# Attention and gated MLP on one core: the order of the first loads and of the second head group, and four holds on GpSimd

## The chip, the core and the metric

The kernel runs on one core of a Trainium2 chip. The core has five engines with an instruction stream each: TensorE (PE) multiplies matrices, VectorE (DVE) and ScalarE (ACT) work elementwise, GpSimd (POOL) works elementwise and issues DMAs, and SyncE (SP) issues DMAs. Every engine executes its own stream in order and waits on semaphores for the others, so an instruction that waits holds back everything behind it on its engine. The metric is the time on the device in microseconds (us), as the median of several runs. Before the change it is 300.85 us, from six runs between 299.44 and 302.98.

## What is computed

Attention with normalised queries and keys is followed by a gated MLP. Shapes: batch 8, 12 heads, sequence 448, head dimension 64; model width 768, two halves of 512 in the MLP.

```python
q_n, k_n = rmsnorm(q, g_q), rmsnorm(k, g_k)         # x / sqrt(mean(x*x) + 1e-6) * g, over the head dimension
scores = (1 / sqrt(64)) * (q_n @ k_n.T)
attn = exp(scores - max) ; attn = attn / (sum(attn) + 1e-9)
x = concat_heads(attn @ v)                          # (8, 448, 768)
h = relu(x @ w_in) ; u, v = h[..., :512], h[..., 512:]
v_n = (v - mean(v)) / sqrt(var(v) + 1e-6)
v_s = einsum('ts,bsd->btd', w_spatial, v_n) + b_spatial
out = (u * v_s) @ w_out
```

## The kernel before, in words

**Groups.** The heads of a batch are split into three groups of four heads: group g of a batch takes heads g and g+3 of the first six and the same of the last six, so that all 128 partitions are used. There are 24 groups G in all: 0, 1, 2 are batch 0, and 3, 4, 5 batch 1. A group is 7 chunks of 128 columns per q and k, and its scores are 7 *passes*: pass p belongs to group p // 7.

**Loading.** `load_part(b, i, part, g)` (L101) issues one DMA for q (i = 0) or k (i = 1) of batch b. The data of one tensor and batch comes in five parts: part 0 the main rows of the first six heads, part 1 their tail, parts 2 and 3 the main rows of the last six in two partition halves, part 4 their tail. With `g` given, parts 0, 2 and 3 bring the two heads of one group only; without, six heads. Parts 1 and 4 always bring six heads. Batch 0 is loaded by groups, every later batch by five whole parts per tensor (`divmod(n, 5)` in L134 and L710). `load_v(b, parts)` (L111) issues the same five parts for v on GpSimd's queue, and `load_w_in(h)` (L186) four DMAs for one half of `w_in`, also on GpSimd. The buffers of two batches alternate: batch 1 has one of its own, batch 2 takes the place of batch 0 and of the early working tiles, once these are read for the last time.

**Preparing a group.** `squares(G, i)` (L223) squares q or k on GpSimd (or ScalarE), `reduce(G, i)` (L236) sums the squares on VectorE, `rstd(G)` (L244) takes the inverse root on ScalarE with two small instructions, `scaled(G, i)` (L252) multiplies q or k by it into bf16 on GpSimd or VectorE. Then the result is turned: by TensorE into PSUM with a copy out of it (`transpose_first` for group 0 in two halves, L283; `transpose_pe` for groups 1 to 5, L302), or by a DMA for later groups (L317), where k is then scaled by `k_scale` (L327). Group 0 is handled in two halves of 4 and 3 chunks (a third entry 0 or 1 in its key); the working tiles of halves come from the pool `first`.

**Scores and attention.** `scores` (L337) multiplies for one pass into PSUM; `expo` (L353) takes exponentials on ScalarE. `weigh(G, part)` (L367) multiplies the exponentials by ones (part -1) or by v (parts 0 and 1); `recip` (L383) and `xt_store` (L389) divide by the sum.

**Order.** The order on every engine is written out by hand. For passes 0 to 19 the loop at L680 issues `expo(p)`, transposes named in `TURN`, the scores of pass p + 1, and then what `early(p)` (L635) lists for that pass; `attend_late` (L404) spreads the attention of groups 0 and 1 over passes 10 to 13 and 15 to 18. From pass 20 on the loop at L750 works in steps of two passes with one exponential of double width; the first is step 10. What a step prepares stands in the table `todo`: it is filled from `EVEN`, `ODD` and `FIRST` (for groups 4 to 8) and with the loads of batches 2 and later. MLP work is filled in between the attention of later groups by a list of small units (`gated`, `fill`).

**The hold.** `after(key)` (L594) copies one element of a scaled tile on GpSimd. GpSimd thus waits there until the scaling has written it:

```python
def after(key):
    t = st_pool.tile([1, 1], BF, name="one")
    pool.tensor_copy(out=t, in_=nrm[key][0:1, 0, 0, 0:1])
```

Before the change it is called for both halves of group 0 and for group 1.

Of the kernel before, what the change touches and what calls it, by code (L numbers as in the profile page):

```python
# [11 lines left out]
BF = mybir.dt.bfloat16  # L12
# [7 lines left out]
def kernel(  # L20
# [24 lines left out]
    P = 128  # L45
    NG = 3
    NCH = 7
# [34 lines left out]
    raw, qbs = {}, {}  # L82

    def load_tile(b, i):
        pl = qb_pools[(b + 1) % 2] if b else first
        t = pl.tile([P, 2 * NG, NCH, D], FP, name="kb" if i else "qb")
        qbs[b, i] = t.rearrange("p h c d -> p h (c d)")
        for g in range(NG):
            x = t.rearrange("p (h g) c d -> p h g c d", g=NG)[:, :, g]
            raw[NG * b + g, i] = x  # L90
            if b == 0 and g == 0:
                raw[0, i, 0], raw[0, i, 1] = x[:, :, 0:4], x[:, :, 4:NCH]

    def pieces(x):

# [3 lines left out]


    def load_part(b, i, part, g=None, eng=sync):  # L101
        if part == 0 and (b, i) not in qbs:
# [8 lines left out]
    def load_v(b, parts):  # L111
        t = vts[b % 2].rearrange("p h c d -> p h (c d)")
        for i in parts:
            hs = slice(6, 12) if i > 1 else slice(0, 6)
            r, c, n, x = pieces(v[b][hs])[i]
            pool.dma_start(out=t[r, hs, D * c:D * (c + n)], in_=x)  # L116
# [9 lines left out]
    load_part(0, 1, 3, 0, act)  # L126
    load_part(0, 0, 4)
    load_part(0, 1, 4, None, act)
    for g in (1, 2):
        for i in (1, 0):  # L130
            for part in (0, 2):
                load_part(0, i, part, g)
    for n in range(10):
        load_part(1, *divmod(n, 5))  # L134


    ident = const.tile([P, P], BF)
# [48 lines left out]
    def load_w_in(h):  # L186
        w = w_in_v if h else w_in_u
        for l in range(4):
            pool.dma_start(
                out=w[32 * l:32 * l + 32, :, :],  # L190
                in_=moe_w_in[192 * l:192 * l + 192, DH * h:DH * h + DH].rearrange("(j p) f -> p j f", p=32))
# [31 lines left out]
    def squares(*key, eng=None):  # L223
        n = nch(key)
        if n == NCH:
            t = sq_pool.tile([P, 2, n, D], FP, name="sqt")
        else:
            t = first.tile([P, 2, n, D], FP, name=f"s{key[1]}{key[2]}")
        x = raw[key]
        if eng is act:  # L230
            act.activation(out=t, in_=x, func=AF.Square, bias=0.0, scale=1.0)
        else:
            pool.tensor_tensor(out=t, in0=x, in1=x, op=ALU.mult)  # L233
        sqt[key] = t

    def reduce(*key):  # L236
        n = nch(key)
        gk = (key[0],) + key[2:]
        if gk not in sqs:
            sqs[gk] = st_pool.tile([P, 2, 2 * n], FP, name=f"ms{n}")  # L240
        dve.tensor_reduce(out=sqs[gk][:, key[1], :], in_=sqt.pop(key).rearrange("p h c d -> p (h c) d"),  # L241
                          axis=AX.X, op=ALU.add)

    def rstd(*gk):  # L244
        t = sqs[gk]
        n = t.shape[-1]
        ln = st_pool.tile([P, 2, n], FP, name=f"ln{n}")
        rst[gk] = st_pool.tile([P, 2, n], FP, name=f"rs{n}")
        act.activation(out=ln, in_=t, func=AF.Ln, bias=eps, scale=1.0 / D)
        act.activation(out=rst[gk], in_=ln, func=AF.Exp, bias=0.0, scale=-0.5)  # L250

    def scaled(*key, eng=None):  # L252
        n = nch(key)
        if n == NCH:
            t = qn_pool.tile([P, n, 2, D], BF, name=f"n{key[1]}")
        else:
            t = first.tile([P, n, 2, D], BF, name=f"n{key[1]}{key[2]}")
        nrm[key] = t
        gk = (key[0],) + key[2:]
        (eng or pool).tensor_tensor(  # L260
            out=t.rearrange("p c h d -> p h c d"), in0=raw[key],
            in1=rst[gk][:, key[1], :].rearrange("p (h c) -> p h c", h=2).to_broadcast([P, 2, n, D]),
            op=ALU.mult)
# [19 lines left out]
    def transpose_first(i, y, eng):  # L283
        ps = ps_w.tile([P, 8, 128], BF, name="ps")
        if y == 0:
            t = first.tile([P, 512], BF, name=f"x{i}")
            turn(ps, 0, nrm[0, i, 0])
            (to_k if i else to_q)(t, ps, 4, eng)
        else:

            n = 3 if i else 4
            t = first.tile([P, 128 * n], BF, name=f"y{i}")
            if i == 0:
                turn(ps, 0, nrm[0, 0, 0][:, 3:4])
            turn(ps, n - 3, nrm[0, i, 1])
            (to_k if i else to_q)(t, ps, n, eng)
        if i == 0:
            qkt[0, 0, y] = t[:, 64 * y:64 * y + S]
        else:
            qkt[0, 1, y] = t  # L300

    def transpose_pe(G, i, eng):  # L302
# [309 lines left out]
    scaled(0, 1, 0, eng=dve)  # L612
    dve.tensor_copy(out=g2_col, in_=ps_g[:, 0:1])
    transpose_first(0, 0, act)
    squares(1, 0, eng=act)
    after((0, 1, 0))
    squares(1, 1)
    transpose_first(1, 0, dve)
    dummies(10)
    reduce(0, 1, 1)  # L620
    rstd(0, 1)
    reduce(1, 1)
    scaled(0, 0, 1, eng=dve)
    scaled(0, 1, 1, eng=dve)
    after((0, 1, 1))
    load_v(0, range(5))

    psp = {}

# [5 lines left out]
    def early(p):  # L635
        if p == 0:
            transpose_first(0, 1, dve)
            transpose_first(1, 1, dve)
            reduce(1, 0)
        elif p == 3:  # L640
            rstd(1)
            scaled(1, 0, eng=dve)
            scaled(1, 1, eng=dve)
            after((1, 1))
            squares(2, 1)
            load_w_in(1)
        elif p == 4:
            squares(2, 0, eng=act)
        elif p == 6:
            reduce(2, 1)  # L650
            reduce(2, 0)
        elif p == 8:
            rstd(2)
            scaled(2, 0, eng=dve)
            scaled(2, 1)
            squares(3, 0)
            squares(3, 1)
            load_v(1, range(5))
# [12 lines left out]
        if 10 <= p <= 13:  # L671
            attend_late(0, p - 10)
        if 15 <= p <= 18:
            attend_late(1, p - 15)
        if p in (0, 1, 2, 3, 4, 7, 8, 9, 14):
            dummies(6)

    TURN = {5: (1, 0), 6: (1, 1), 11: (2, 0), 12: (2, 1), 18: (3, 0), 19: (3, 1)}
    pass_scores(0)
    for p in range(2 * S0):  # L680
        expo(psp[p], p, 1)
        if p in TURN:
            transpose_pe(*TURN[p], dve)
        if p + 1 < 2 * S0:
            pass_scores(p + 1)
        early(p)
# [10 lines left out]
    todo = {}  # L697
# [8 lines left out]
                        todo.setdefault(s, []).append((what, G, i))  # L706
    for b in range(2, B):
        first_q = {2: S0, 3: 16}.get(b, (21 * b - 36) // 2)
        for n in range(10):
            todo.setdefault(first_q + n // (3 if b > 2 else 4), []).append(("ld", NG * b, n))  # L710

    ORDER = ("ks", "red", "rstd", "sc", "sq", "turn", "tr", "ld")

    def prep(s, early_act):
        for what, G, i in sorted(todo.get(s, ()), key=lambda x: (ORDER.index(x[0]), x[1:])):
            if (what == "rstd" and G < 5) != early_act:
                continue
            if what == "ld":
                load_part(G // NG, *divmod(i, 5))
            elif what == "turn":  # L720
                transpose_pe(G, i, dve)
            elif what == "sq":
                squares(G, i, eng=act if (G, i) in ((6, 1), (7, 1), (8, 1)) else None)
            elif what == "red":
                reduce(G, i)
            elif what == "rstd":
                rstd(G)
            elif what == "sc":
                scaled(G, i, eng=dve if (G, i) in ((4, 0), (5, 0)) else None)
            elif what == "tr":  # L730
                transpose_dma(G, i)
            elif what == "ks":
                k_scale(G)
# [86 lines left out]
```

## Time and profile before

| | |
|---|---|
| median of six runs | 300.85 us |
| the profiled execution: time / span of its trace | 301.68 / 299.8 us |
| busy: TensorE, VectorE, ScalarE, GpSimd | 92%, 70%, 68%, 67% of the span |
| data moved by DMA | 49.98 MB, 167 GB/s over the span |
| mean granted TensorE clock | 0.966 |

The profile page divides the span into 40 slices of 7.5 us; a digit is the busy share in tenths, 9 being 90% or more. "PEclk" is the TensorE clock that was granted, DMA the mean busy share of the core's 16 DMA engines:

```profile
PE   8675797979896999999999999999999999999994
DVE  3874355868746976996899686877897949644652
ACT  2687376597874787688677768867877876774421
POOL 3677299278994989958989989589989860400400
PEclk9799577999799999999999999999999999999999
```

Row by row: TensorE is almost full from the fourteenth slice (97.5 us) on, and has gaps before. In the fifth slice (30 to 37.5 us) ScalarE and GpSimd are at a few tenths, and TensorE's clock is granted at half. Bracketed remarks in later excerpts name the idle time of the engine just before an instruction and what ended it.

### The profile page before, as it was taken

To read this page: it belongs to the slowest core of one execution; us is meant where nothing else is said; L and a number is where in the kernel's file an instruction comes from. 1 tells how busy PE (TensorE), PEld (TensorE's weight loads), DVE (VectorE), ACT (ScalarE), POOL (GpSimd) and SP (SyncE) were. 2 spreads that over 40 slices of the span, in tenths; PEclk is the share of its full clock that TensorE was granted. 3 is DMA by queue.
4 is the path that set the end of the run, shared out by engine and by line. 5 is a ranking of instruction groups with operands and counts; after the bars stand their busy time and mean duration, and the time that the engine had idled before them with its cause. 6 is when DMAs were issued, how large, how long until landed. Compare 5 with 4: busy or idle time off the path is not lost.

```text
span 299.8 us, 6418 instructions
## 1 busy us (share of the span) xinstructions
PE 274.4 (92%) x2541; PEld 128.9 (43%) x2541; DVE 210.6 (70%) x363; ACT 204.7 (68%) x258; POOL 202.3 (67%) x188
## 2 busy tenths in 40 slices
PE   8675797979896999999999999999999999999994
PEld 8342233434342444444444444444344444444552
DVE  3874355868746976996899686877897949644652
ACT  2687376597874787688677768867877876774421
POOL 3677299278994989958989989589989860400400
PEclk9799577999799999999999999999999999999999
DMA  7999999447999999999979999999891794040145
GB/s 166 242 217 227 227 208 203 68 105 163 155 202 195 200 196 188 217 248 162 255 103 181 242 209 239 247 177 166 167 121 39 113 197 92 2 157 2 26 161 184
DMA packets 97120, 49.98 MB, mean 167 GB/s; under 512 B 67009, under 2 KB 93378, under 8 KB 97090
## 3 DMA queue, kind: packets, MB, share of 16 engines
q1 hardware_dynamic: 73986, 40.32, 64.2%
q0 software_dynamic: 21744, 8.66, 25.0%
q10 hardware_dynamic: 1360, 0.59, 0.8%
q8 instruction: 20, 0.33, 0.5%
q14 instruction: 10, 0.08, 0.1%
HBM read 38.55 MB, written 11.01 MB: 165 GB/s over the span
## 4 chain that ended last, share of the span: by engine, by line
PE 61%; DMA 13%; DVE 9%; ACT 8%; POOL 5%; issue 3%; SPq 0%; ACTq 0%; POOLq 0%; DVEq 0%
PE ps L379 13%; PE ps L458 11%; PE ps L530 10%; PE ps L488 9%; PE pss L350 8%; PE ps L498 7%; ACT et L357 5%; DMA kr<-n 5%; DMA vt<-in_v_dram 5%; DMA kb<-in_k_dram 3%; DVE ms L241 2%; DVE xt L393 2%; DVE kT L330 2%; PE pss L346 1%; POOL n L260 1%
## 5 line engine op out<-in xcount | busy, mean ns | idle before, releaser
L357 ACT ACTIVATE et<-pss 128x1792 bf16<-128x1792 f32 x74 | 123.0, 1663 | 51.2 <-PE pss L350 48.4
L393 DVE TENSOR_TENSOR xt<-ps,rc 128x448 bf16<-128x448 f32 x48 | 28.0, 619 | 35.7 <-ACT rc L386 31.3
L241 DVE TENSOR_REDUCE ms<-sqt 128x14 f32<-128x896 f32 x46 | 49.2, 1076 | 2.9 <-POOL sqt L233 2.5
L530 PE MATMUL ps<-w_out,gt 128*128 128x384 bf16 (+1 forms) x256 | 46.9, 327 | 0.9 <-DVE osb L435 0.4
L379 PE MATMUL ps<-et,vt 128*32 128x448 bf16 x768 | 44.0, 368 | 3.4 <-DMA vt<-in_v_dram 2.9
L458 PE MATMUL ps<-w_in_v,xt 128*128 128x512 bf16 (+1 forms) x192 | 45.6, 380 | 0.0
L260 POOL TENSOR_TENSOR n<-qb,rs 128x896 bf16<-128x896 f32 x18 | 30.4, 1687 | 21.0 <-ACT rs L250 17.2
L260 POOL TENSOR_TENSOR n<-kb,rs 128x896 bf16<-128x896 f32 x22 | 39.0, 1773 | 7.4 <-ACT rs L250 7.3
L350 PE MATMUL pss<-qT,kT 64*128 64x448 bf16 x254 | 37.5, 356 | 7.1 <-ACT et L357 4.4
L488 PE MATMUL ps<-xt,w_in_u 128*128 128x448 bf16 x192 | 40.1, 353 | 1.3 <-DVE vs L429 0.8
L233 POOL TENSOR_TENSOR sqt<-kb 128x896 f32<-128x896 f32 x20 | 33.6, 1682 | 6.7 <-DMA kb<-in_k_dram 6.5
L233 POOL TENSOR_TENSOR sqt<-qb 128x896 f32<-128x896 f32 x21 | 35.3, 1683 | 0.1
L530 PEld LDWEIGHTS <-gt 128*128 128x128 bf16 (+1 forms) x256 | 24.1, 101 | 21.1 <-issue 8.3
L435 DVE COPY osb<-ps 128x384 f32<-128x384 f32 (+1 forms) x46 | 25.1, 555 | 10.2 <-PE ps L530 9.2
L379 PEld LDWEIGHTS <-vt 128*32 128x32 bf16 x768 | 21.4, 100 | 21.4 <-issue 6.5
L116 POOL DMA_DIRECT2D vt<-in_v_dram x40 | 29.3, 738 | 0.0
L480 POOL TENSOR_SCALAR vn<-vs,nm,rv 128x512 bf16<-128x512 bf16 (+1 forms) x32 | 24.1, 769 | 7.2 <-issue 4.3
L498 PE MATMUL ps<-w_spT,vn 128*128 128x448 bf16 (+1 forms) x128 | 28.3, 365 | 0.2 <-DVE w_spT L209 0.2
L488 PEld LDWEIGHTS <-w_in_u 128*128 128x128 bf16 x192 | 17.3, 98 | 21.5 <-issue 7.6
L350 PEld LDWEIGHTS <-kT 64*128 64x128 bf16 x276 | 10.1, 94 | 37.3 <-issue 28.8
L458 PEld LDWEIGHTS <-xt 128*128 128x128 bf16 (+1 forms) x192 | 17.8, 100 | 18.3 <-issue 3.6
L330 DVE TENSOR_SCALAR_CACHE_REDUCE kT<-kr,g_col 128x896 bf16<-128x896 bf16 x18 | 20.5, 1136 | 4.1 <-DMA kr<-n 4.1
(86 smaller groups left out, 314.8 us busy)
## 6 DMA issues: line engine op xcount, KB each, us to landing
out_dram<-osb SPq DMA_DIRECT2D x24, 384.0 KB, 4.5
qb<-in_q_dram SPq DMA_DIRECT2D x7, 576.0 KB, 6.1
qb<-in_q_dram SPq DMA_DIRECT2D x14, 288.0 KB, 6.5
kb<-in_k_dram SPq DMA_DIRECT2D x7, 576.0 KB, 8.7
kb<-in_k_dram SPq DMA_DIRECT2D x14, 288.0 KB, 8.6
vt<-in_v_dram POOLq DMA_DIRECT2D x8, 288.0 KB, 6.0
vt<-in_v_dram POOLq DMA_DIRECT2D x16, 144.0 KB, 5.3
qb<-in_q_dram SPq DMA_DIRECT2D x20, 96.0 KB, 6.0
```

The lines of the kernel that those rows point to most:

```text
L116: pool.dma_start(out=t[r, hs, D * c:D * (c + n)], in_=x)
L233: pool.tensor_tensor(out=t, in0=x, in1=x, op=ALU.mult)
L241: dve.tensor_reduce(out=sqs[gk][:, key[1], :], in_=sqt.pop(key).rearrange("p h c d -> p (h c) d"), axis=AX.X, op=ALU.add)
L260: (eng or pool).tensor_tensor(out=t.rearrange("p c h d -> p h c d"), in0=raw[key], in1=rst[gk][:, key[1], :].rearrange("p (h c) -> p h c", ...
L350: pe.matmul(out=ps[:, h, 0:S], lhsT=kT[r, c0:c0 + 128], rhs=qT[r, :], start=True, stop=True, tile_position=(64 * h, 0))
L357: act.activation(out=ets[s][:, 2 * a:2 * a + 2 * m, :], in_=ps[:, 0:2 * m, 0:S], func=AF.Exp, bias=0.0, scale=1.0)
L379: pe.matmul(out=ps[32 * l:32 * l + 32, 0:S], lhsT=w, rhs=et_of(G, 3 if r == 3 else r + 4 * y, h), start=(r == 0), stop=(r == 3), tile_posi ...
L393: dve.tensor_tensor(out=xts[b][:, 2 * g + half, :], in0=pst.pop((G, half))[:, 0:S], in1=rec[G], op=ALU.mult)
L458: pe.matmul(out=ps[0:m, :], lhsT=xts[b][:, j, t0:t0 + m], rhs=w_in_v[:, j, :], start=(j == 0), stop=(j == 5), tile_position=(0, 0))
L488: pe.matmul(out=ps[:, 0:S], lhsT=w_in_u[:, j, 128 * f:128 * f + 128], rhs=xts[b][:, j, :], start=(j == 0), stop=(j == 5))
L498: pe.matmul(out=ps[:, 0:S], lhsT=vn_t[b % 2][0:kp, c, 128 * f:128 * f + 128], rhs=w_spT[0:kp, c, :], start=(c == 0), stop=(c == NT - 1))
L530: pe.matmul(out=ps[o:o + m, 0:384], lhsT=gts[b][f][:, t0:t0 + m], rhs=w_out[:, f, r], start=(f == 0), stop=(f == 3), tile_position=(0, o))
```

## The change

It has six parts, in the order of the program:

1. *Group 1 in halves.* Group 1 of batch 0 is now squared, summed, scaled and turned in two halves of 4 and 3 chunks, as group 0 was. Its first half is squared on ScalarE, q as well as k. A new helper, `transpose_half`, turns one half.
2. *Order of batch 0's loads.* Within group 1, k and q alternate by part; group 2 keeps tensor by tensor.
3. *v of batch 0 ahead of batch 1.* Two of the five v loads are issued before the second hold, the other three right behind it. Batch 1's q and k loads come later in the program, and the first of them has to wait for a one-element memset that GpSimd executes behind the second hold, ahead of the three v loads. SyncE's queue is in order, so all of batch 1 waits with it.
4. *Batches 1 and 2 by groups.* 22 loads per batch in place of 10: k and q of the batch's first group with the tails, then its second and third group.
5. *Passes 1 to 19 in a new order.* Scaling of group 2's and group 3's k goes from GpSimd to VectorE; `squares(2, 0)` goes from ScalarE to GpSimd; copies of the turned q of groups 2 and 3 go from VectorE to ScalarE, and both tensors of a group are turned in the same pass (13 and 19, where it was 11/12 and 18/19). Loads of `w_in` and of batch 1's v are issued in later passes.
6. *Four holds.* `after` is called behind the scaling of group 1's two halves, of group 2 and of group 3; before it was called behind group 1 as a whole. The two calls for group 0 stay.

```diff
@@ load_tile
-            if b == 0 and g == 0:
-                raw[0, i, 0], raw[0, i, 1] = x[:, :, 0:4], x[:, :, 4:NCH]
+            if b == 0 and g < 2:
+                raw[g, i, 0], raw[g, i, 1] = x[:, :, 0:4], x[:, :, 4:NCH]
@@ first loads
-    for g in (1, 2):
+    for part in (0, 2):
         for i in (1, 0):
-            for part in (0, 2):
-                load_part(0, i, part, g)
-    for n in range(10):
-        load_part(1, *divmod(n, 5))
+            load_part(0, i, part, 1)
+    for i in (1, 0):
+        for part in (0, 2):
+            load_part(0, i, part, 2)
+
+    BY_GROUP = [(i, part, None if part in (1, 4) else g)
+                for g in range(NG) for i in (1, 0) for part in ((0, 2, 3) if g else (0, 2, 3, 1, 4))]
@@ new helper
+    def transpose_half(G, i, y, eng):
+        ps = ps_w.tile([P, 8, 128], BF, name="ps")
+        turn(ps, 0, nrm[G, i, y])
+        if y == 0:
+            halves[G, i] = qt_pool.tile([P, NCH * 128], BF, name="kT" if i else "qT")
+            put(G, i, halves[G, i])
+        n = 3 if y else 4
+        (to_k if i else to_q)(halves[G, i][:, 512 * y:512 * y + 128 * n], ps, n, eng)
@@ before the passes
-    squares(1, 0, eng=act)
+    squares(1, 1, 0, eng=act)
+    squares(1, 0, 0, eng=act)
     after((0, 1, 0))
-    squares(1, 1)
+    load_v(0, (0, 1))
...
-    reduce(1, 1)
+    reduce(1, 1, 0)
     scaled(0, 0, 1, eng=dve)
     scaled(0, 1, 1, eng=dve)
+    reduce(1, 0, 0)
     after((0, 1, 1))
-    load_v(0, range(5))
+
+    load_tile(1, 1)
+    pool.memset(raw[NG, 1][0:1, 0, 0, 0:1], 0.0)
+    for x in BY_GROUP:
+        load_part(1, *x)
+    load_v(0, (2, 3, 4))
@@ early(p)
-            reduce(1, 0)
-        elif p == 3:
-            rstd(1)
-            scaled(1, 0, eng=dve)
-            scaled(1, 1, eng=dve)
-            after((1, 1))
+        elif p == 1:
+            rstd(1, 0)
+            scaled(1, 0, 0, eng=dve)
+            scaled(1, 1, 0, eng=dve)
+            after((1, 1, 0))
+            squares(1, 1, 1)
+            squares(1, 0, 1)
             squares(2, 1)
-            load_w_in(1)
         elif p == 4:
-            squares(2, 0, eng=act)
+            transpose_half(1, 0, 0, dve)
+            transpose_half(1, 1, 0, dve)
+            reduce(1, 1, 1)
+            reduce(1, 0, 1)
         elif p == 6:
+            rstd(1, 1)
+            scaled(1, 0, 1, eng=dve)
+            scaled(1, 1, 1, eng=dve)
+            after((1, 1, 1))
+            squares(2, 0)
+            squares(3, 1)
+        elif p == 8:
+            transpose_half(1, 0, 1, dve)
+            transpose_half(1, 1, 1, dve)
             reduce(2, 1)
             reduce(2, 0)
-        elif p == 8:
+        elif p == 11:
             rstd(2)
             scaled(2, 0, eng=dve)
-            scaled(2, 1)
+            scaled(2, 1, eng=dve)
+            after((2, 1))
             squares(3, 0)
-            squares(3, 1)
-            load_v(1, range(5))
+            load_w_in(1)
         elif p == 14:
+            reduce(3, 1)
             reduce(3, 0)
-            reduce(3, 1)
-        elif p == 16:
+            squares(4, 0)
+        elif p == 18:
             rstd(3)
             scaled(3, 0, eng=dve)
-            scaled(3, 1)
-            squares(4, 0)
+            scaled(3, 1, eng=dve)
+            after((3, 1))
             squares(4, 1)
+            load_v(1, range(5))
             load_w_in(0)
@@ passes
-    TURN = {5: (1, 0), 6: (1, 1), 11: (2, 0), 12: (2, 1), 18: (3, 0), 19: (3, 1)}
+    TURN = {13: 2, 19: 3}
...
         if p in TURN:
-            transpose_pe(*TURN[p], dve)
+            transpose_pe(TURN[p], 0, act)
+            transpose_pe(TURN[p], 1, dve)
@@ later loads
-        for n in range(10):
-            todo.setdefault(first_q + n // (3 if b > 2 else 4), []).append(("ld", NG * b, n))
+        for n, x in enumerate(BY_GROUP if b == 2 else [divmod(n, 5) for n in range(10)]):
+            todo.setdefault(first_q + n // (3 if b > 2 else 4), []).append(("ld", NG * b, x))
```

Two lines in `prep` follow from the last edit (the entry of a load is now a tuple and is passed on as it is, in the order of the list).

More of the change, by code (lines that the diff above doesn't have):

```diff
@@ L101, in load_part @@
     def load_part(b, i, part, g=None, eng=sync):
-        if part == 0 and (b, i) not in qbs:
+        if (b, i) not in qbs:
             load_tile(b, i)
@@ L300, in transpose_first @@
             qkt[0, 1, y] = t
+    halves = {}
+    def transpose_half(G, i, y, eng):
[6 more added lines that the diff above has]
+        (to_k if i else to_q)(halves[G, i][:, 512 * y:512 * y + 128 * n], ps, n, eng)
     def transpose_pe(G, i, eng):
@@ L708 @@
         first_q = {2: S0, 3: 16}.get(b, (21 * b - 36) // 2)
-        for n in range(10):
-            todo.setdefault(first_q + n // (3 if b > 2 else 4), []).append(("ld", NG * b, n))
+        for n, x in enumerate(BY_GROUP if b == 2 else [divmod(n, 5) for n in range(10)]):
+            todo.setdefault(first_q + n // (3 if b > 2 else 4), []).append(("ld", NG * b, x))
     ORDER = ("ks", "red", "rstd", "sc", "sq", "turn", "tr", "ld")
     def prep(s, early_act):
-        for what, G, i in sorted(todo.get(s, ()), key=lambda x: (ORDER.index(x[0]), x[1:])):
+        for what, G, i in sorted(todo.get(s, ()), key=lambda x: (ORDER.index(x[0]), x[1:2] if x[0] == "ld" else x[1:])):
             if (what == "rstd" and G < 5) != early_act:
@@ L718, in prep @@
             if what == "ld":
-                load_part(G // NG, *divmod(i, 5))
+                load_part(G // NG, *i)
             elif what == "turn":
```

## The prediction

> **What bounds the kernel now.** I read three views in this order: the slices and the table of windows (where TensorE is not full), the timeline there (what it waits for), the chain of waits (whether that sets the end). The windows' columns are start:end, length, busy us (and instructions) of TensorE, its weight loads, VectorE, ScalarE and GpSimd, then granted clock, DMA share, GB/s.
>
> ```profile
> 30.00:34.00 4.00, 2.98 (x27) 1.08 (x30) 0.66 (x2) 0.00 (x0) 0.00 (x0) 0.60 1.19 217
> 34.00:46.00 12.00, 10.25 (x102) 3.88 (x95) 7.69 (x12) 8.97 (x13) 10.30 (x10) 0.71 1.28 221
> 46.00:60.00 14.00, 12.80 (x112) 5.49 (x115) 9.69 (x16) 8.45 (x10) 8.68 (x9) 0.88 0.78 127
> 60.00:100.00 40.00, 33.52 (x344) 15.60 (x336) 27.87 (x47) 30.39 (x39) 32.01 (x26) 0.96 0.93 168
> 100.00:273.00 173.00, 171.30 (x1626) 76.19 (x1622) 133.85 (x231) 131.35 (x154) 129.49 (x111) 1.00 0.94 167
> ```
>
> From 100 to 273 us TensorE is busy 171.3 of 173.0: nothing can be won there, and what is won before it arrives at the end. The place to look is the start. From 30 to 34 us ScalarE and GpSimd do nothing at all. The timeline says why (start, length, instruction, idle time before it and what ended it):
>
> ```profile
> 15.05 3.53 POOL L116 DMA_DIRECT2D vt<-in_v_dram  x5
> 25.08 0.57 POOL L189 DMA_DIRECT2D w_in_v<-in_moe_w_in_dram  x1 [1.23 <-DMA vt<-in_v_dram]
> 29.91 0.56 PE L379 MATMUL ps<-et,vt 128*32 128x448 bf16 x8 [1.88 <-DMA vt<-in_v_dram]
> 31.50 0.93 PE L379 MATMUL ps<-et,vt 128*32 128x448 bf16 x6 [1.02 <-DMA vt<-in_v_dram]
> 34.69 3.35 ACT L357 ACTIVATE et<-pse 128x896 bf16<-128x896 f32 x4 [6.37 <-PE ps L379]
> 35.70 1.68 POOL L233 TENSOR_TENSOR sqt<-kb 128x896 f32<-128x896 f32 x1 [6.54 <-DMA kb<-in_k_dram]
> ```
>
> GpSimd issues v of batch 0 at 15.05, when SyncE has already queued batch 1's q and k. TensorE starts `weigh(0, 0)` at 27.67 and gets through only at 31.5; ScalarE stands 6.37 us. The chain of waits agrees, so the stall sets the end:
>
> ```profile
> 15.11 2.76 POOL vt L116 x4
> 17.87 13.59 DMA vt<-in_v_dram
> 31.50 0.93 PE ps L379 x6
> ```
>
> **v first, batch 1 held back.** Two v pieces go out behind `after((0, 1, 0))` (its copy runs at 10.85 now), three behind `after((0, 1, 1))` (14.93 now), together with a one-element memset that batch 1's first k load must wait for. Packets decide the cost: in the first 30 us the DMA view counts 11,632, or 388 per us. q and k of a batch are 4,608 packets, v is 2,304. Batch 0 and the two v pieces: 4,608+1,152 = 5,760, done at 14.8 us, so the gate opens just as the engines would run dry: cost about 0. The other v pieces (1,152) at half share against batch 1 take 2,304/388 = 5.9 us: about 21, at v's worst delay in the trace (13.6 us) 30. My walk below needs them at 25.
>
> **Batches 1 and 2 by groups.** 22 loads replace 10, twice; bytes and packets are the same. The Trainium skill ("DMA: Bandwidth & Descriptors", section "Anatomy of one DMA") puts about 2.0 us of fixed cost on a DMA: 24 more of them would be 48 us if it were paid in turn, and group 3 would be late. The rows:
>
> ```profile
> qb<-in_q_dram SPq DMA_DIRECT2D x14, 288.0 KB, 6.5
> qb<-in_q_dram SPq DMA_DIRECT2D x20, 96.0 KB, 6.0
> ```
>
> A third of the bytes lands hardly sooner, so there is a fixed part, but pieces overlap: SyncE issues two small ones in 1.25 us (8.37), so 22 take 13.7 us where batch 1's ten took 5.1+8.0 = 13.1. I take 0. Eight loads are in flight at most (each waits for the semaphore of the eighth before it); at 6 to 8 us each, group 3's ten land by 24 to 28, and squares(3, 0) starts at 28.3.
>
> **Group 1 in halves, more on VectorE.** Squares of 512 cost ScalarE 0.63 each, two for one of 0.95: +0.3, but squares(2, 0) leaves it (-0.94) and two qT copies come (512 columns took 0.60, so an estimate of 0.95 each): with one rstd pair more (+0.52) +1.8 in all. VectorE takes scaled(2, 1) and (3, 1) (+1.08 each). VectorE has room (7.69 of 12), so only the order counts. I walked passes 0 to 19 with the trace's durations (score exponential 0.86 apart, reduce 1.07, scaling 1.09 or 0.69/0.55 for halves, GpSimd square 1.68, recip 1.14): pass 0 at 13.4; rstd(1, 0) at 15.0; half 0 of kT ready 18.8, pass 7 at 20.4; half 1 ready 22.9, pass 10 at 23.6; rstd(2) 25.4, scaled(2, 1) ends 28.1; pass 14 at 30.1 (it waits for kT of group 2); rstd(3) 35.5, scaled(3, 1) ends 38.2; kT of group 3 at 39.5; first double exponential at 40.2, where the trace has 45.49. **The stall's 6.4 us come back, less 1.1 of new order: 5.3 us by step 10.**
>
> **The four holds.** `after` makes GpSimd wait for VectorE's scaling. The skill ("SBUF — State Buffer", section "SBUF: two separate sides") calls their common port an exclusive lock: whoever starts first blocks the other for the whole instruction. The trace shows one side:
>
> ```profile
> 61.90 1.09 DVE L260 TENSOR_TENSOR n<-qb,rs 128x896 bf16<-128x896 f32 x1
> 61.95 2.59 POOL L260 TENSOR_TENSOR n<-kb,rs 128x896 bf16<-128x896 f32 x1 [7.26 <-ACT rs L250]
> ```
>
> VectorE first: GpSimd takes 2.59 instead of 1.69 and VectorE loses nothing. GpSimd first is shown nowhere before; by the rule a square could delay a scaling by up to 1.68, by the row by 0. I count the holds as no gain. Their price is GpSimd's queue: behind the last one (38.2, after some 4 us idle) stand squares(4, 1), five v loads of batch 1 (3.53), four of w_in_u (2.29), scaled(4, 1), squares(5, 0) and (5, 1).
>
> **Where part is given back.** squares(4, 1) ends at 40.1; v out until 43.7; w_in_u from there. GpSimd's loads too share eight semaphores: the fourth w_in_u load waits for the landing of the first v piece (the 1.23 us wait at 25.08 above is this kind). Before, three computations lay between and no wait shows; now they follow at once. With L the delay of that v piece, issued at 40.2, squares(5, 0) ends at 40.2+L+0.6+1.7+1.7 and its reduce starts at about 44.3+L. That reduce is in VectorE's order ahead of group 4's copies:
>
> ```profile
> 52.42 1.07 DVE L241 TENSOR_REDUCE ms<-sqt 128x14 f32<-128x896 f32 x1
> 53.41 0.61 DVE L274 COPY qT<-ps 128x896 bf16<-128x896 bf16 x1
> 53.94 1.08 DVE L241 TENSOR_REDUCE ms<-sqt 128x14 f32<-128x896 f32 x1
> 56.11 0.68 DVE L281 TENSOR_SCALAR kT<-ps,g_col 128x896 bf16<-128x896 bf16 x1 [1.09 <-PE ps L267]
> ```
>
> Shifted by 5.3 it should start at 47.1, and VectorE would stand. From here it is nearly solid to 65 us, with gaps of 1.09 and 0.89 and about half a us of other slack: 2.5 in all. So gain = min(5.3, 52.4 - (44.3+L) + 2.5) = min(5.3, 10.6 - L). L: 6.0 is the median of such v pieces in the whole trace, 9.7 to 13.6 the spread of the first ten, beside loads six heads wide, and the first of batch 1's lies between 9.7 and 10.1 (it was down when the fourth w_in_u load went out). By packets: at 40.2 some 15,600 have moved, 1,300 of batch 2 are left, plus 768 of the piece and some 300 beside: 6.1 us and 1 for the start. I take 7.5, nearer the packets since batch 2 is further ahead, and get **3.1 us**. GpSimd then finds its rhythm again in the 7.26 us gap before 61.95, and from 100 us the gain stands.
>
> **Sum.** The profiled execution took 301.68 us (span 299.8 and 1.9 around it); less 3.1 is 298.6. It lies 0.8 above the median 300.85, so for the median of the new kernel I say **297.8**.
>
> **Rivals.**
> 1. *All is kept* (L below 6): 300.85 - 5.3 = 295.6. For it: from 100 us on there is no other limit, and a warmer clock (0.71 in 34 to 46 us) could add. Against it: every v piece of the first 50 us took 9.7 or more.
> 2. *The gain is hidden* (L of 9.1 to 12.1, as the nearest row has it, or group 3's data late by three): at L = 10, 0.6 us, 300.2.
> 3. *Slower: GpSimd's queue at the fourth w_in_u load.* At L = 13.6, the trace's maximum, the reduce starts at 57.9, the formula gives -3.0: 303.9. It decides from L = 10.6, and shows above 12.1. For it: v pieces took that long beside q and k; against it: the queue of batch 2 is eight small loads deep, not ten wide ones.
>
> **Numbers.** Half a per cent, 1.5 us, is what a measurement of this kernel tells from no change. Forecast (gain 1.5 to 4.5) 0.50; rival 1 0.22; rival 2 0.16; rival 3 0.12. So faster 0.72, same 0.16, slower 0.12. The range 295.2 to 301.0 holds the forecast, rival 1 and most of rival 2; it leaves rival 3 and a little at the low end.
>
> **What would show it.** Right: no idle ahead of `weigh(0, 0)` for v; first double exponential near 40; GpSimd waiting at the last w_in_u load near 46 for v; VectorE's reduce of group 5 waiting for GpSimd's square near 49 to 52. Wrong: the first double exponential later than 42 (the walk failed: look for k of group 3 or a v piece behind it), or no wait at w_in_u (rival 1), or TensorE waiting near 55 for v or w_in_u.

## The result, and the profile after

The median is 300.37 us (34 runs, 297.26 to 302.91); before, in the same sessions, it was 301.51 (71 runs). **The ratio is 0.9959, 95% interval 0.9939 to 0.9979**: a gain of 0.6 to 1.8 us, where 3.1 were forecast. Ratios, here and below, leave out a kernel's slow executions, those more than 1.5% above its fastest. The profiled execution took 299.74 us with a span of 298.0, which is 1.94 less than the one before.

Four of the page's rows by slices (40 of 7.45 us) answer to those of before:

```profile
PE   8588659968968999999999989999999999999994
ACT  2779856659854797678779767967787876674421
POOL 3765678588994899859979889589989850400400
PEclk9879969999997999999999999999999999999999
```

The hole in ScalarE and GpSimd in the fifth slice is filled. TensorE's hole in the thirteenth slice of before (90 to 97.5 us, a 6) now stands in the twelfth (82 to 89 us), and this time the clock is at 7 in the slice behind it. In the table of windows (start:end, length, busy us of TensorE, its weight loads, VectorE, ScalarE, GpSimd, clock, DMA share, GB/s):

```profile
30.00:34.00 4.00, 2.91 (x44) 1.36 (x48) 3.17 (x4) 3.19 (x5) 4.00 (x6) 1.00 0.74 155
...
60.00:100.00 40.00, 32.34 (x302) 14.67 (x302) 29.49 (x48) 27.84 (x35) 32.20 (x26) 0.96 1.03 180
100.00:271.00 171.00, 168.81 (x1608) 75.13 (x1609) 131.01 (x224) 129.47 (x153) 126.67 (x110) 1.00 0.93 165
```

From 30 to 34 us the engines work now. From 60 to 100 us, though, TensorE stands idle for 7.7 of the 40 us, where it was 6.5 before: that is where to look for what is missing.

A step table shows it best: the start of each exponential of double width, read from the timeline of both traces. Step s holds passes 2s and 2s + 1.

| step | before | after | difference |
|---|---|---|---|
| 10 | 45.49 | 40.98 | -4.51 |
| 14 | 59.74 | 55.17 | -4.57 |
| 17 | 70.13 | 66.60 | -3.53 |
| 20 | 79.50 | 76.05 | -3.45 |
| 23 | 88.78 | 84.20 | -4.58 |
| 24 | 94.14 | 91.32 | -2.82 |
| 25 | 96.80 | 95.25 | -1.55 |
| 26 | 100.58 | 98.24 | -2.34 |
| 51 | 173.04 | 170.71 | -2.33 |
| 52 | 176.21 | 174.37 | -1.84 |
| 83 (last) | 269.11 | 267.26 | -1.85 |

The gain is made by step 10 and stands at 4.6 us in step 23; in between, from step 17 to 20, it is 1.1 smaller. Then 2.2 of it go within three steps, and 0.5 at step 52. All losses lie where a new group begins: step 17 holds the first pass of group 5, step 24 of group 7, step 52 of group 15.

**Up to step 14** the timeline of after (start, length, instruction, idle time before it and what ended it) shows what the prediction said:

```profile
26.01 0.94 PE L394 MATMUL ps<-et,vt 128*32 128x448 bf16 x16
38.97 0.18 POOL L612 COPY one<-n 1x1 bf16<-1x1 bf16 x1 [4.19 <-DVE n L264]
47.16 0.57 POOL L193 DMA_DIRECT2D w_in_u<-in_moe_w_in_dram  x1 [1.18 <-DMA vt<-in_v_dram]
51.11 1.08 DVE L245 TENSOR_REDUCE ms<-sqt 128x14 f32<-128x896 f32 x1 [3.17 <-POOL sqt L237]
```

The product with v no longer waits. GpSimd waits at the fourth hold, later at the last `w_in_u` load for v, and VectorE's reduce for GpSimd's square.

**At step 17** GpSimd comes first and VectorE pays. The timeline of after:

```profile
59.09 4.16 POOL L237 TENSOR_TENSOR sqt<-qb 128x896 f32<-128x896 f32 x2
59.39 2.31 DVE L264 TENSOR_TENSOR n<-qb,rs 128x896 bf16<-128x896 f32 x1
```

The scaling of group 5's q took 1.09 before (the row at 61.90 in the prediction); it takes 2.31 here, beside squares that take 4.16 for two. VectorE had been busy without a gap since the late reduce (51.11) and came to the scaling when GpSimd's own scaling (57.44) was over and its squares had begun. TensorE's transposes of group 5, and with them step 17, wait for this scaling.

**At step 24** TensorE waits for k of group 7, which a DMA turns. The timeline of after, then that of before, then one line of each kernel's chain of waits (start, length, what; after first):

```profile
89.51 1.15 DVE L345 TENSOR_SCALAR_CACHE_REDUCE kT<-kr,g_col 128x896 bf16<-128x896 bf16 x1 [5.33 <-DMA kr<-n]
...
90.72 0.56 PE L365 MATMUL pss<-qT,kT 64*128 64x448 bf16 x2 [4.01 <-DVE kT L345]
```

```profile
93.74 0.36 PE L350 MATMUL pss<-qT,kT 64*128 64x448 bf16 x2 [2.44 <-DVE kT L330]
```

```profile
80.22 9.26 DMA kr<-n
```

```profile
83.71 8.79 DMA kr<-n
```

The wait was there before the change, on the chain that sets the end. The transfer's issue comes only 3.49 us earlier, because GpSimd's scaling of group 7 still carries the loss of step 17 (step 20: -3.45), and it is 0.47 longer in flight. So TensorE arrives 4.58 earlier and is let go 3.02 earlier.

**At step 25** the clock adds to it. The windows of after:

```profile
85.00:90.00 5.00, 1.72 (x9) 0.55 (x7) 0.49 (x1) 1.35 (x2) 4.07 (x4) 1.00 1.36 188
90.00:95.00 5.00, 4.28 (x23) 1.83 (x23) 4.90 (x10) 2.10 (x3) 1.42 (x1) 0.66 1.05 228
```

After the idle time the granted clock is 0.66, and two score multiplications take 0.56 for 0.36. In the kernel before, the shorter wait (2.44 us, up to 93.74) left it at 1.00 from 90 to 95 us and from 95 to 100 us.

The account of the two traces: -4.58 at step 23; +1.09 that the issue of the transposing DMA kept from step 17; +0.47 for its longer flight; +0.20 at step 24 and +1.27 at step 25, where the clock is low (a run below takes this apart); -0.79 won back at step 26; +0.49 at step 52. The sum is -1.85.

### The profile page after: what moved, and what is told of

It is laid out like the page before. It is cut to its first block, busy times and chain, and to the rows that moved or that the text cites. A ratio compares the mean times of both kernels' runs of the same rounds, so it can differ in the third digit from the quotient of the medians.

```text
span 298.0 us, 6482 instructions
## 1 busy us (share of the span) xinstructions
PE 270.6 (91%) x2541; PEld 126.9 (43%) x2541; DVE 212.8 (71%) x369; ACT 206.5 (69%) x262; POOL 200.3 (67%) x192
## 4 chain that ended last, share of the span: by engine, by line
PE 60%; DMA 13%; DVE 11%; ACT 8%; POOL 3%; issue 2%; SPq 2%; ACTq 0%; POOLq 0%; DVEq 0%
PE ps L394 11%; PE ps L545 10%; PE ps L473 10%; PE ps L503 10%; PE pss L365 7%; PE ps L513 7%; ACT et L372 5%; DMA kr<-n 5%; DMA qb<-in_q_dram 5%; DVE ms L245 3%; DMA kb<-in_k_dram 3%; DVE xt L408 2%; SPq L107 2%; DVE kT L345 2%; POOL n L264 1%
## 5 line engine op out<-in xcount | busy, mean ns | idle before, releaser
L245 DVE TENSOR_REDUCE ms<-sqt 128x14 f32<-128x896 f32 x44 | 47.0, 1075 | 3.6 <-POOL sqt L237 3.2
L545 PE MATMUL ps<-w_out,gt 128*128 128x384 bf16 (+1 forms) x256 | 47.6, 330 | 1.4 <-DVE osb L450 0.9
L473 PE MATMUL ps<-w_in_v,xt 128*128 128x512 bf16 (+1 forms) x192 | 46.8, 388 | 0.0
L365 PE MATMUL pss<-qT,kT 64*128 64x448 bf16 x254 | 38.2, 362 | 8.2 <-DVE kT L345 4.0
L394 PE MATMUL ps<-et,vt 128*32 128x448 bf16 x768 | 41.4, 356 | 0.0
L237 POOL TENSOR_TENSOR sqt<-qb 128x896 f32<-128x896 f32 x22 | 37.9, 1723 | 0.2
L264 POOL TENSOR_TENSOR n<-kb,rs 128x896 bf16<-128x896 f32 x20 | 33.9, 1696 | 3.8 <-issue 3.6
L237 POOL TENSOR_TENSOR sqt<-kb 128x896 f32<-128x896 f32 x19 | 31.9, 1681 | 0.3 <-DVE xt L408 0.2
L513 PE MATMUL ps<-w_spT,vn 128*128 128x448 bf16 (+1 forms) x128 | 27.2, 353 | 0.4 <-DVE w_spT L213 0.4
L394 PEld LDWEIGHTS <-vt 128*32 128x32 bf16 x768 | 20.4, 98 | 16.5 <-issue 1.9
```

Of the source, the lines that this page charges most:

```text
L264: (eng or pool).tensor_tensor(out=t.rearrange("p c h d -> p h c d"), in0=raw[key], in1=rst[gk][:, key[1], :].rearrange("p (h c) -> p h c", ...
L365: pe.matmul(out=ps[:, h, 0:S], lhsT=kT[r, c0:c0 + 128], rhs=qT[r, :], start=True, stop=True, tile_position=(64 * h, 0))
L394: pe.matmul(out=ps[32 * l:32 * l + 32, 0:S], lhsT=w, rhs=et_of(G, 3 if r == 3 else r + 4 * y, h), start=(r == 0), stop=(r == 3), tile_posi ...
L473: pe.matmul(out=ps[0:m, :], lhsT=xts[b][:, j, t0:t0 + m], rhs=w_in_v[:, j, :], start=(j == 0), stop=(j == 5), tile_position=(0, 0))
L513: pe.matmul(out=ps[:, 0:S], lhsT=vn_t[b % 2][0:kp, c, 128 * f:128 * f + 128], rhs=w_spT[0:kp, c, :], start=(c == 0), stop=(c == NT - 1))
L545: pe.matmul(out=ps[o:o + m, 0:384], lhsT=gts[b][f][:, t0:t0 + m], rhs=w_out[:, f, r], start=(f == 0), stop=(f == 3), tile_position=(0, o))
```

## Experiments

Twelve kernels, with ratios against the kernel before in the same session. Differences of steps are against the trace of before unless another is named.

**The holds taken away** (the four `after` calls of the change go; those of group 0 stay):

```diff
-            after((1, 1, 0))
...
-            after((1, 1, 1))
...
-            after((2, 1))
...
-            after((3, 1))
```

> The changed kernel without its four new holds (the two of group 0 stay). Theory A: where a GpSimd square is under way when VectorE's scaling comes, the scaling takes up to 1.7 us longer; at least two of the six scalings of groups 1 to 3 are longer than 1.3 us (halves 0.9), and step 10 comes 1 to 3 us later than in the changed kernel; the end is 0 to 2 us later, ratio 0.996 to 1.003. Theory C: GpSimd is 2 to 4 us earlier at its loads in pass 18, no scaling is longer, step 10 is as early as in the changed kernel, and the end 1 us earlier, ratio 0.993.

Measured: ratio 1.0224 (1.0168 to 1.028), step 10 at +2.79, 7.3 later than with the holds. The timeline:

```profile
15.65 5.90 DVE L264 TENSOR_TENSOR n<-kb,rs 128x512 bf16<-128x512 f32 x1
16.09 0.87 POOL L237 TENSOR_TENSOR s<-kb 128x384 f32<-128x384 f32 x1
16.88 0.86 POOL L237 TENSOR_TENSOR s<-qb 128x384 f32<-128x384 f32 x1
17.66 1.70 POOL L237 TENSOR_TENSOR sqt<-kb 128x896 f32<-128x896 f32 x1
19.30 1.70 POOL L237 TENSOR_TENSOR sqt<-qb 128x896 f32<-128x896 f32 x1
```

A scaling that takes 0.68 with the hold (at 15.75 in the trace of after) takes 5.90. It ends only when GpSimd's four squares are over (at 21.0). Group 2's two scalings take 2.25 and 2.56 for 1.09. The loss is larger than either theory had it. The holds are what makes the reordering pay; the prediction counted them "as no gain".

**v ahead of batch 1, alone, in the kernel before:**

```diff
-    for n in range(10):
-        load_part(1, *divmod(n, 5))
...
     squares(1, 1)
+    load_v(0, (0, 1))
...
-    load_v(0, range(5))
+    load_tile(1, 0)
+    pool.memset(raw[NG, 0][0:1, 0, 0, 0:1], 0.0)
+    for n in range(10):
+        load_part(1, *divmod(n, 5))
+    load_v(0, (2, 3, 4))
```

> The kernel before with the first part of the change alone: v of batch 0 goes ahead of batch 1 (two pieces, then the gate by a one-element memset, then three), batch 1 stays in ten whole loads, everything else as before. If v first is what wins at the start: TensorE's wait for v at 27.7 us goes, step 10 comes 3 to 5 us earlier. If the loads by groups and the new order are needed as well: k of batch 1, last in its queue, still lands at 35 to 38 us, the stall moves to squares(3, 1), and step 10 is within 1.5 us of before. Ratio in the first case 0.985 to 0.993, in the second 0.995 to 1.005.

Measured: 1.0115 (1.0061 to 1.0168), slower than either case; step 10 at +1.63. TensorE no longer waits for v. What is left is GpSimd's wait for k of group 3, which the kernel before had as well (6.54 us, ended at 35.70) and which now ends 2.2 us later:

```profile
37.89 1.68 POOL L230 TENSOR_TENSOR sqt<-kb 128x896 f32<-128x896 f32 x1 [7.67 <-DMA kb<-in_k_dram]
```

Of the 3.2 us by which this trace ends later, 2.3 come at step 24, behind a turned k that is 9.8 us in flight. So this part by itself makes the kernel slower; it needs the loads of batch 1 by groups, or the new order, or both (which of them was not tried apart).

**Batch 2 in ten whole loads**, the rest as changed:

```diff
-        for n, x in enumerate(BY_GROUP if b == 2 else [divmod(n, 5) for n in range(10)]):
+        for n, x in enumerate([divmod(n, 5) for n in range(10)]):
```

> The changed kernel with batch 2 loaded as before, in ten loads of six heads (batch 1 stays by groups). Theory A: batch 2 is far from the path, so steps 10 to 26 move by less than 0.5 us and the ratio stays at 0.995 to 0.997. Theory B: SyncE is through earlier, batch 3's loads and the transposes of step 20 have the DMA engines to themselves, and the loss at step 24 falls by 1 to 2 us: ratio 0.989 to 0.993.

Measured: 1.0101 (1.006 to 1.0142); step 10 at -5.38, step 14 at -2.33. The timeline has the cause:

```profile
49.50 0.57 POOL L193 DMA_DIRECT2D w_in_u<-in_moe_w_in_dram  x1 [4.12 <-DMA vt<-in_v_dram]
...
53.45 1.09 DVE L245 TENSOR_REDUCE ms<-sqt 128x14 f32<-128x896 f32 x1 [5.42 <-POOL sqt L237]
```

The first v piece of batch 1, issued at 40.17, lands by 49.50: 9.3 us, where the changed kernel has 6.4 (40.76 to 47.16). This is the prediction's L, and min(5.3, 10.6 - L) at 9.3 is 1.3; the gain at step 14 is 2.33. From step 10 to 14 this trace loses 3.05 us and that of the changed kernel nothing: 2.9 us more of L cost 3.1, so the slope of the formula is shown, and its offset is a microsecond off. Both theories were wrong: batch 2 by small loads was costed at 0 and brings about 1.4%. The edit changes two things at once, though: the loads are larger, and more of batch 2 is queued early. SyncE has handed over all of it by 43.8 us, where in the changed kernel the last three loads go out from 45.4 on; from 40.8 to 47 us, beside the v piece, SyncE's queue moves 1,928 packets, where the changed kernel has 1,323. Whether the size of the loads counts or the bytes already queued ahead of v was not tried apart.

**v of batch 1 issued earlier**, at pass 14 instead of 18:

```diff
             squares(4, 0)
+            load_v(1, range(5))
...
             squares(4, 1)
-            load_v(1, range(5))
```

> The changed kernel with one edit: the five v loads of batch 1 are issued in pass 14, ahead of the hold behind group 3, and no longer in pass 18 behind it. Theory A (what was won by step 14 is lost in two later places: at step 17, because GpSimd's loads make VectorE late and its scaling of group 5's q then lies behind a GpSimd square; and at step 24, where group 7's turned k is late by DMA): the wait of VectorE for squares(5, 0) falls from 3.2 to under 0.5 us, the scaling takes 1.1 instead of 2.3, step 17 is 4.5 ahead of the kernel before instead of 3.5; step 24 gains at most 1 us of it, so the time is 0 to 1 us below the changed kernel, ratio to before 0.993 to 0.996. Theory B (the loads of batch 2 by groups keep SyncE and the DMA engines late): the scaling stays long or not, but the end does not move, 0.996. Theory C (the holds themselves cost): no change either.

Measured: 0.9906 (0.987 to 0.9941). The reduce of group 5 starts at 49.78 without a wait, and VectorE comes first at the scaling:

```profile
59.30 1.09 DVE L264 TENSOR_TENSOR n<-qb,rs 128x896 bf16<-128x896 f32 x1
```

The collision is gone, as the first theory said. The trace happened to have a low clock (0.66 from 40 to 50 us and 0.79 from 60 to 65, where before has 0.84 and 1.00), so its steps cannot be set against those of after one by one (step 17 loses 0.6 here, without the collision); the ratio lies a little over half a per cent below that of the changed kernel, and the two intervals just touch.

**The DMA queues quiet at the turned k.** w_out (768 KB) and v of batch 2 leave the stretch from 70 to 90 us for the one from 50 to 60, where the kernel before moves about 100 GB/s or less:

```diff
-            v_step.update({s + 6 + i: (b + 2, [i]) for i in range(5)})
+            v_step.update({13: (2, [0, 1]), 14: (2, [2, 3, 4])} if b == 0 else {s + 6 + i: (b + 2, [i]) for i in range(5)})
...
-        if s == 19:
+        if s == 13:
             load_w_out()
```

> The changed kernel with v of batch 2 and w_out loaded in steps 13 and 14, where the DMA engines are half idle, and no longer in steps 18 to 22, where group 7's k is turned by DMA. Theory A: the transposed k lands in 4 to 7 us instead of 9.3, TensorE's wait at step 24 falls from 4.0 to under 1.5 us and its clock stays full there; step 26 is 3.5 to 4.5 ahead of the kernel before instead of 2.3, the time 1.5 to 2.2 us below the changed kernel, ratio 0.989 to 0.991. Theory B: the transposes wait for batch 3's q and k, not for v and w_out, so step 24 keeps a wait of 3 us or more, ratio 0.995 to 0.997. Theory C: no change.

Measured: 293.86 us, **0.978 (0.9736 to 0.9824)**. The turned k, issued at 78.44, is down before VectorE asks for it, as the timeline shows by the missing bracket:

```profile
83.10 1.14 DVE L345 TENSOR_SCALAR_CACHE_REDUCE kT<-kr,g_col 128x896 bf16<-128x896 bf16 x1
```

At most 4.7 us in flight, for 9.26. The gain is more than either theory expected. Step 24 stands at -7.92, step 26 at -8.71, the end at -8.29. About two of these were there before step 10, where this edit does nothing: that is how far two traces differ early on. The collision at step 17 is still there (2.56).

The same edit in the kernel **before**:

> The kernel before with v of batch 2 and w_out in steps 13 and 14, nothing else. It tells whether the change's gain is real once step 24 no longer takes it. Theory A: the kernel before loses its own wait of 2.4 us at step 24, so it gains 2 to 3.5 us, ratio 0.988 to 0.993; the changed kernel with the same edit, 0.978, is then 3 to 4.5 us better, as it was by step 14. If instead the edit alone makes the whole gain and the change none, this kernel reaches 0.978 to 0.981 as well.

Measured: 0.9854 (0.9798 to 0.9909), end at -4.3, and no wait for the turned k at step 24:

```profile
87.45 1.14 DVE L330 TENSOR_SCALAR_CACHE_REDUCE kT<-kr,g_col 128x896 bf16<-128x896 bf16 x1
```

So the floor at step 24 belonged to the kernel before as well. With it out of the way the change is worth 0.978 / 0.9854 = 0.9925, or 2.2 us; the half-widths 0.0044 and 0.0056 together give it an uncertainty of 0.007, 2.1 us, so by time alone 2.2 cannot be told from the 1.2 with the floor in place. The steps tell more. Between the traces of the two quiet kernels the gain is 5.2 us at step 10, 5.1 at step 16, 4.0 at step 17, 4.1 at steps 24 and 26 and 4.0 at the end: step 24 takes nothing from it. What step 17 takes stays lost.

**Both edits together** (v of batch 1 early, the queues quiet):

> The changed kernel with both edits of the runs before: v of batch 1 in pass 14, v of batch 2 and w_out in steps 13 and 14. Theory A: the scaling of group 5's q takes 1.1 us, and no transposed k is late at step 24; 0.5 to 1.2 us below the run with the second edit alone, ratio 0.974 to 0.977. If the two edits get in each other's way (DMA engines full where v of batch 1 now lies): 0 to 1 us above it, 0.978 to 0.982.

Measured: 0.980 (0.9753 to 0.9847), scaling 1.09, no wait at step 24: the intervals of this and of the quiet kernel overlap almost wholly. What the collision at step 17 costs once step 24 is clear is not settled: the time shows no gain from its absence, and in this trace a low clock (0.66 from 60 to 65 us) lengthens the same step, as the transposes of group 5 take 1.68 us for 1.08.

**Only w_out moved:**

```diff
-        if s == 19:
+        if s == 13:
             load_w_out()
```

> After, with only the load of w_out moved from step 19 to step 13. Theory A: each of the two transfers that lie on the DMA engines between 70 and 90 us (w_out, 0.79 MB, and v of batch 2, 0.69 MB) delays the turned k of group 7 by its share, so this run gets about half of what the two edits together gave (0.9959 to 0.978): ratio 0.985 to 0.989, TensorE's wait at step 24 between 1.5 and 2.8 us where the changed kernel has 4.0. Theory B: w_out alone does it, since it is issued next to the turned k: ratio about 0.980, wait below 1.0. Theory C: it is v of batch 2 alone: ratio about 0.996, wait still near 4.

Measured: 0.9937 (0.9894 to 0.998). Against the changed kernel's trace, step 24 comes 4.40 earlier and TensorE does not wait there: that is the second theory, by its wait, though the ratio is far from its 0.980. The turned k is issued 0.80 us earlier (79.42), because w_out's issue no longer stands ahead of its scaling on GpSimd, and is 5.1 us in flight for 9.26. But at step 31, the first pass of group 9, 4.1 of it are lost, and the timeline names the same kind of wait:

```profile
104.81 1.15 DVE L345 TENSOR_SCALAR_CACHE_REDUCE kT<-kr,g_col 128x896 bf16<-128x896 bf16 x1 [2.60 <-DMA kr<-n]
```

That transfer was 7.5 us in flight (from 97.33). With v moved as well it does not wait. The turned k of group 9 is a floor of its own, and what passes the one of group 7 meets it.

**Only v of batch 2 moved:**

```diff
-            v_step.update({s + 6 + i: (b + 2, [i]) for i in range(5)})
+            v_step.update({13: (2, [0, 1]), 14: (2, [2, 3, 4])} if b == 0 else {s + 6 + i: (b + 2, [i]) for i in range(5)})
```

> After, with only v of batch 2 moved ahead, to steps 13 and 14. Theory A: half of the gain, ratio 0.985 to 0.989, wait at step 24 between 1.5 and 2.8 us. Theory B (w_out alone): ratio about 0.996 and a wait near 4. Theory C (v of batch 2 alone): ratio about 0.980, wait below 1.0.

Inconclusive by time: six runs from 293.81 to 303.16, median 300.54 beside 301.4 before, too far apart for a ratio. In the trace w_out is 13.7 us in flight, the turned k 12.1, and TensorE waits at step 24:

```profile
93.06 0.55 PE L365 MATMUL pss<-qT,kT 64*128 64x448 bf16 x2 [5.30 <-DVE kT L345]
```

So v alone does not clear it. Why one run reached 293.81 was not found.

**A fifth hold** in the quiet kernel, for the collision at step 17; first behind GpSimd's scaling of group 5's k, then ahead of it:

```diff
                 scaled(G, i, eng=dve if (G, i) in ((4, 0), (5, 0)) else None)
+                if (G, i) == (5, 1):
+                    after((5, 0))
```

> The changed kernel with v of batch 2 and w_out in steps 13 and 14 and a fifth hold: GpSimd waits for VectorE's scaling of group 5's q before squares(6, 0). If the collision at step 17 is the cause of the 1 us lost there: the scaling falls from 2.6 to 1.1 us, step 17 comes 0.6 to 1.2 us earlier against step 16, the time 0.5 to 1 us below the run without the hold, 0.974 to 0.977. If GpSimd's own delay takes it back: the same 0.978 within its interval.

Measured: 0.9772 (0.9717 to 0.9826), scaling 2.01: it lay behind GpSimd's own scaling (56.74 to 58.4) now, so the hold was too late to tell anything.

```diff
+                if (G, i) == (5, 1):
+                    after((5, 0))
                 scaled(G, i, eng=dve if (G, i) in ((4, 0), (5, 0)) else None)
```

> The kernel with both transfers moved, and a fifth hold on GpSimd, this time ahead of its own scaling of group 5's k (the hold of the earlier run stood behind it). Theory A (GpSimd's long instruction, once begun, blocks VectorE): the scaling of group 5's q takes 1.09 us where it took 2.56, step 17 starts 1.0 to 1.4 us earlier against step 16 than there; ratio 0.974 to 0.978, because step 21 had made up for the loss in the changed kernel anyway and little of it reaches the end. Theory B (the loss at step 17 reaches the end once step 24 is clear): 0.972 to 0.975. If the hold delays GpSimd's squares for group 6 so much that they are late, it is above 0.980.

Measured: 0.9854 (0.9782 to 0.9926). The scaling takes 1.09 (at 57.59), and yet step 17 comes 2.0 later against step 16 than in the quiet kernel:

```profile
58.74 0.18 POOL L612 COPY one<-n 1x1 bf16<-1x1 bf16 x1 [4.03 <-DVE n L264]
...
62.25 2.08 DVE L245 TENSOR_REDUCE ms<-sqt 128x14 f32<-128x896 f32 x2 [2.50 <-POOL sqt L237]
```

GpSimd stands 4.03 us, its square of group 6 is late, and VectorE waits 2.50 for that: the third case of the expectation. In this trace, a hold on an engine whose results the other needs next gives back more than the collision costs; the intervals of the two ratios overlap, so the time doesn't show it.

**TensorE kept busy** in the wait at step 24, by 40 extra multiplications whose result is not used:

```diff
+        if s == 24:
+            ps_f = ps_w.tile([P, 512], FP, name="ps")
+            for _ in range(40):
+                pe.matmul(out=ps_f[:, 0:128], lhsT=ident, rhs=ident, start=True, stop=True)
         scores(pss[:, 0:2], 2 * s)
```

> After, with 40 extra multiplications of 128 columns (result unused) ahead of the scores of step 24, so that TensorE is busy while it waits for the turned k. Theory A (the further 1.27 us lost at step 25 are the lower clock that follows the idle time): step 24 starts within 0.5 us of where the changed kernel has it, the granted clock from 90 to 95 us is 0.9 or more where it was 0.66, step 25 comes 0.8 to 1.3 us earlier; ratio 0.991 to 0.994. Theory B (step 25 is late for its own data): clock up but step 25 unchanged, ratio 0.995 to 0.998. If the extra work runs past the arrival of the turned k it costs up to 1 us.

Measured: 0.9976 (0.993 to 1.0022). The windows have the clock at full where it was 0.66:

```profile
90.00:95.00 5.00, 4.05 (x38) 1.75 (x38) 4.67 (x8) 2.09 (x3) 0.83 (x1) 1.00 1.29 192
```

Steps 24 and 25 are 3.17 us apart, where after has 3.93 and before 2.66. So about 0.76 of the 1.27 goes with the low clock; the rest stays open. By step 26 only -0.5 is left relative to step 24, and the ratio cannot be told from that of the changed kernel; theory A had expected 0.991 to 0.994.

## Why the prediction was wrong

By its own steps:

- **The stall on v and what it set free: right.** The walk said pass 0 at 13.4, the last scaling of group 3 done at 38.2 and the first double exponential at 40.2; measured 12.77, 38.9 and 40.98. The 5.3 us by step 10 are 4.5: this term was 0.8 too large.
- **v first and batch 1 held back, cost about 0: right in the whole, but not by itself.** Alone, in the kernel before, it costs 1.15%.
- **Batches 1 and 2 by groups, cost 0: wrong in sign, for batch 2.** With them L is 6.4 us, with whole loads 9.3. The page "DMA: Bandwidth & Descriptors" of the Trainium skill, section "Anatomy of one DMA", gives its fixed cost of some 2 us for a DMA that GpSimd issues, and the 24 extra ones are SyncE's, so the prediction's 48 us carried the figure over to another queue. Nothing of the kind was paid: the run with whole loads of batch 2 is the slower one.
- **The holds, "no gain": wrong.** Without them the kernel has 1.0224 of the time before, with them 0.9959. The rule of the page "SBUF — State Buffer", section "SBUF: two separate sides", of one engine blocking the other until its instruction is over, fits step 17 (a scaling 1.2 us longer beside a square of 1.6 us) but not the run without holds: there VectorE had begun first by the record, and it lost 5.2 us over four squares, three times the 1.68 that was taken as the bound. This did not move the forecast, since the holds are in the kernel.
- **The v piece and the formula 10.6 - L: right in the waits, the size by luck.** Every wait named beforehand is there. L was taken as 7.5 and is 6.4, which makes 4.2, and the step table has 4.57. But the formula takes these 4.2 from 5.3 by a loss of 1.1 between step 10 and 14, and the table has 4.51 at step 10 and loses nothing: two errors of about a microsecond cancel.
- **"GpSimd then finds its rhythm again in the 7.26 us gap before 61.95, and from 100 us the gain stands": this step failed.** GpSimd does not wait for VectorE there but runs ahead of it, and VectorE's scaling loses 1.2 us to it. Then the turned k of group 7, which TensorE had waited 2.44 us for already, holds step 24: its issue is tied to GpSimd's queue and its flight to w_out, and neither moves with TensorE. 4.58 us arrived at that floor, 2.34 passed it, and 1.85 are left at the end. That the floor takes the 2.2 is shown by the quiet kernels: the wait goes when w_out is out of its way, and then the 4.1 us that stand at step 23 stand at step 24 as well. That the loss at step 17 is due to the collision rests on the order of the rows there; the runs made for it (v early, fifth hold) do not settle it.

The mistake could have been seen: the chain of waits of before has the turned k of group 7 with 8.79 us, the largest piece after the first 50 us, and TensorE's row with 2.44 of idle time is in its timeline; the prediction's own table of windows had 6.5 us of idle TensorE from 60 to 100 us. I stopped following the chain where the early stretch ended, and took TensorE's full row from 100 us on as proof that nothing lay between. Rival 2 ("the gain is hidden") had the size nearly right for the wrong reason: it needed an L of 9.1 to 12.1. That the median of 300.37 lies within 295.2 to 301.0 is owed to that rival's share of the range, not to the mechanism.

The 0.49 at step 52 look like a third floor of this kind: the chains of both kernels have the turned k of group 15 with 5.9 us, issued at 165.98 before and at 164.15 after, only 1.83 earlier where TensorE is 2.33 earlier. No run took that apart, so this stays a guess. Open, too, is why the flight of a turned k differs from run to run.

## What to carry to other kernels

A gain at the start of a kernel arrives at the end only past every later floor: follow the chain of waits to its last wait and ask, for each transfer on it, what its issue hangs on and what shares the DMA engines with it. Large loads that nobody needs yet belong into the stretch where the DMA engines idle; here two such moves alone brought more than the whole change (0.9854 in the kernel before, against 0.9959). A hold that keeps GpSimd off while VectorE runs a two-input operation paid here where GpSimd was ahead of its users; where VectorE needed GpSimd's result next it cost more than it saved, in one trace.

## What the hardware showed

- A VectorE scaling of 0.68 us took 5.90 while GpSimd ran four squares in a row, although by the record it had begun 0.4 us before the first of them. One GpSimd instruction is not the bound on such a delay.
- The same turning DMA was 8.8 to 9.3 us in flight beside w_out and v, and at most 4.7 without them; 5.1 beside v alone, 12.1 beside w_out alone.
- After 4 us of idle TensorE the granted clock was 0.66 over the next 5 us window; with filler work there it stayed at 1.00. After 2.44 us of idle time it stayed at 1.00 too.
- With 22 small loads of the next batch in place of ten large ones, a transfer on another queue took 6.4 us for 9.3; beside it (40.8 to 47 us) the queue of those loads moved 1,323 packets for 1,928.
